# Loading K and V of two heads with one transfer in a decode attention kernel

## The chip, the cores and the metric

The kernel runs on one core of a Trainium2 chip; the chip's other cores are not used by it. The metric is device time in microseconds (us) of one execution. Three runs of the kernel before took 389.30, 389.39 and 389.51 us, median 389.39. A profile is one further execution, recorded by the hardware; its times are counted from its first instruction.

Engines are named as in the profile: PE does matrix products (PEld loads its stationary operand), DVE works on vectors, ACT evaluates functions, POOL does general work, and SP does nothing here but ask for transfers, in one fixed order.

## The reference

Four sequences decode one token each. The layer is attention over a window of the cache and then a gated feed-forward, both with a residual and a normalization without weights:

```
B, D = 4, 576;  Hq, Hkv, Sk, Dh = 32, 16, 16384, 128;  W = 4096;  F = 4608
q = (layernorm(x) @ wq)                        # 32 heads of 128
k = k_cache[:, :, Sk - W:, :]                  # bfloat16, each head serves two q heads
p = softmax(q . k * Dh**-0.5)                  # over the 4096 positions
h = x + (p . v) @ wo
gate, up = layernorm(h) @ W_gate, layernorm(h) @ W_up
out = h + (gate * (gate > 0) * up) @ W_down
```

There are 4 x 16 = 64 heads of K and of V, each 4096 x 128 in bfloat16, 1 MB. They are 134.2 MB of the 159.6 MB that the kernel reads; the rest are the five weight matrices. In memory the window of one head is contiguous, and two neighbouring heads of a sequence begin 16384 x 128 x 2 bytes = 4 MiB apart.

## The kernel before

The program for each engine is written out by hand. A small recorder (`Sched`, L48) notes which instruction signals what, and puts a semaphore wait in front of an instruction for each thing that it depends on. All transfers are asked for by SP in one list (`transfers`, L179, walked by `prog_sync`, L242): an entry first waits until the consumer of what its slot held before is done, and whatever stands behind it in the list waits with it.

The list is: wq in five pieces (L205 to L208); then for m from 0 to 68 K of head m (if there is one) and V of head m - 5 (`VLEAD`, L209 to L213); then wo in four pieces (L216), gate and up (L221, L226) and down (L234). K has a ring of six slots and V one of ten, each of 9216 bytes per partition, in one buffer, `pool` (L120). A slot of K comes free when the head has been transposed, one of V when its PV product is done. One K or V transfer is 1024 KB: partition p takes positions 32p to 32p + 31 of the head, a run of 8192 bytes (L195 to L203). wo comes with two runs of 4608 bytes per partition, gate and up with one run of 9216.

One head goes through these steps:

- **K transpose** (`tr`, L376, the instruction at L382): DVE transposes the 32 x 32 blocks of the head, seen as float32 pairs, from the slot into one of three buffers `kT` (`NKT`). It waits for the data and for the scores of three heads earlier.
- **Scores** (`qk`, L497): eight matmuls of 512 columns add up in two PSUM banks. Four heads form a batch n (`NB`): the stationary operand `qz` of a head is zero but for the columns of its own two q heads, so that the four heads of a batch accumulate into the same two banks on different rows. There are two such pairs of banks, `sc[0]` and `sc[1]` (L167), used in turn: batch n waits for the exponentials of batch n - 2.
- **Maximum and bias** (`rmax` L384, `fbias` L391): DVE takes the maximum of 1024 columns, masks it (`pmax`), POOL combines the partitions (L268), and DVE forms `t` and the `bias`, one number per row.
- **Exponentials** (L314): ACT, two of 512 columns each, with their sums.
- **P transpose** (`trp`, L397): DVE, and two small operations for the row sums; then ACT copies the result to `prob` as bfloat16 (L321).
- **PV** (`pv`, L514): eight matmuls of 512 columns per head, `PVLAG` = 6 heads behind the scores. After four heads ACT copies the result (`cpy`, L297), and `ext` (L526) picks out what belongs to each head.

The order on PE is: scores of head i, then (at a batch's start `ext` of the batch before) PV of head i - 6. The order on DVE around a batch is: K transpose of the batch's last head, maximum and `pmax`; K transpose of the next head, `t` and `bias`; K transpose of the head after, P transpose and row sums. So DVE does one K transpose while POOL works and another while ACT works.

The recorder issues all matmuls from one line, so that nearly all of PE's rows show L469; scores write `sc`, PV and `ext` write `pb`.

After the last batch come the normalized output (`norm`, L406), its product with wo, the second normalization, gate, up and down, all with the weights as the moving or stationary operand in `pool`; the transfers of down wait for the end of the product with wo, since they overwrite its slots.

Of the kernel before, what the change touches and what calls it, by code (L numbers as in the profile page):

```python
# [19 lines left out]
T = WIN // 128  # L20
# [3 lines left out]
NPAIR = B * KVH  # L24
NB = 4
NBATCH = NPAIR // NB
# [3 lines left out]
SLOT = 4608  # L30
NKS = 6
NVS = 10
NSLOT = NKS + NVS
# [3 lines left out]
PVLAG = 6  # L37
# [63 lines left out]
def bass_sequential_preLN__sliding_block_cached__glu_gated_reglu__decode_kernel(  # L101
# [12 lines left out]
    with ExitStack() as es:  # L114
# [4 lines left out]

        pool = sb("pool", [128, NSLOT, SLOT], BF16)  # L120
        kT = sb("kT", [128, NKT, WIN // 2], FP32)
# [20 lines left out]
        mask = sb("mask", [128, 4, 2 * NB], FP32)  # L142
        selT = sb("selT", [128, 4, 2 * NB], FP32)
        rmx = sb("rmx", [128, 2], FP32)
        pmax = sb("pmax", [128, 2, 2 * NB], FP32)
        bcm = sb("bcm", [128, 2, 2 * NB], FP32)
        t8 = sb("t8", [128, 2 * NB], FP32)
        bias = sb("bias", [128, 2], FP32)
        rs2 = sb("rs2", [128, 2, 2], FP32)
# [3 lines left out]
        prob = sb("prob", [128, 3, NB, T, 2], BF16)  # L153
# [13 lines left out]
        sc = [es.enter_context(nc.psum_tensor(f"sc{i}", [128, 1024], FP32)) for i in range(2)]  # L167
        pb = [sc[0][:, 0:512], sc[0][:, 512:1024], sc[1][:, 0:512], sc[1][:, 512:1024]]
# [8 lines left out]
        rings = {"K": [list(range(NKS)), 0], "V": [list(range(NKS, NSLOT)), 0]}  # L177
        slot_user = {}
        transfers = []  # L179
        slot_of = {}  # L180

        def add(name, ring, consumer, make, fixed=None):
            if ring is not None:
                slots, i = rings[ring]
                s = slots[i % len(slots)]
                rings[ring][1] += 1
                free = slot_user.get(s)
                slot_user[s] = consumer
                key = f"slot{s}"
            else:  # L190
                s, free, key = fixed, None, "fix_" + str(name).replace("'", "").replace("(", "").replace(")", "").replace(", ", "_")
            slot_of[name] = s
            transfers.append((name, key, free, lambda e, s=s: make(e, s)))

        def kv(cache, i):  # L195
            b, kvh = divmod(i, KVH)
            return cache[b, kvh, SK - WIN:SK, :].rearrange("(p t) d -> p (t d)", p=128)

        def add_K(i):
            add(("K", i), "K", ("TR", i), lambda e, s: e.dma_start(out=pool[:, s, 0:WIN], in_=kv(A_k_cache, i)))  # L200

        def add_V(i):
            add(("V", i), "V", ("PV", i), lambda e, s: e.dma_start(out=pool[:, s, 0:WIN], in_=kv(A_v_cache, i)))  # L203

        for c in range(4):  # L205
            add(("wq", c), "V", "QMM", lambda e, s, c=c: e.dma_start(out=pool[:, s, 0:H * DH], in_=A_wq[c * 128:(c + 1) * 128, :]))
        add(("wq", 4), "V", "QMM", lambda e, s: e.dma_start(out=pool[:, s, 0:H * DH // 2],
                                                            in_=A_wq[512:576, :].rearrange("r (u n) -> (r u) n", u=2)))  # L208
        for m in range(NPAIR + VLEAD):  # L209
            if m < NPAIR:  # L210
                add_K(m)
            if m >= VLEAD:
                add_V(m - VLEAD)  # L213
        for g in range(NWO):
            add(("wo", g), "K", "ATTN",
                lambda e, s, g=g: e.dma_start(out=pool[:, s, :].rearrange("p (q x) -> p q x", q=2),  # L216
                                              in_=A_wo[g * 1024:(g + 1) * 1024, :].rearrange("(q p e) n -> p q (e n)", q=2, e=4)))
        for c in range(4):
            for kind, W in (("wg", B_W_gate), ("wu", B_W_up)):
                add((kind, c), "V", None,  # L220
                    lambda e, s, c=c, W=W: e.dma_start(out=pool[:, s, 0:F], in_=W[c * 128:(c + 1) * 128, :]))  # L221

        s4 = rings["V"][0][rings["V"][1] % NVS]
        for u, (kind, W) in enumerate((("wg", B_W_gate), ("wu", B_W_up))):
            transfers.append(((kind, 4), f"gu4_{u}", slot_user[s4],
                              lambda e, u=u, W=W: e.dma_start(out=pool[:, s4, u * HALF:(u + 1) * HALF],  # L226
                                                              in_=W[512:576, :].rearrange("r (u n) -> (r u) n", u=2))))
        wd_sb = pool[:, 0:NKS, :].rearrange("p s x -> p (s x)")[:, 0:FC * D].rearrange("p (g x) -> p g x", g=NG)
        WD = [(0, GD * JJ), (GD * JJ, 2 * GD * JJ)] + [(g * JJ, (g + 1) * JJ) for g in range(2 * GD, NG - 1)] + [(FC - JJ, FC - 1), (FC - 1, FC)]
        for k, (f0, f1) in enumerate(WD):  # L230
            g0, j0 = divmod(f0, JJ)
            g1, nj = (f1 // JJ, JJ) if f1 - f0 >= JJ else (g0 + 1, f1 - f0)
            transfers.append((("wd", k), f"wd{k}", "ATTN",
                              lambda e, g0=g0, g1=g1, j0=j0, nj=nj: e.dma_start(  # L234
                                  out=wd_sb[:, g0:g1, j0 * D:(j0 + nj) * D],
                                  in_=B_W_down[g0 * 128 * JJ:g1 * 128 * JJ, :].rearrange("(g p j) n -> p g (j n)", p=128, j=JJ)[:, :, j0 * D:(j0 + nj) * D])))
# [5 lines left out]
        def prog_sync(S):  # L242
            for name, key, free, make in transfers:
                S.dma("sync", make, key, deps=[free], name=land(name))
# [27 lines left out]
        def prog_act(S):  # L272
# [12 lines left out]
            def qzero(n):  # L285
                b, q = divmod(n, 4)
                for g in range(4):
                    deps = []
                    if g == 0:
                        deps = ["D_QR", "QZ0"] if n < 2 else [("QK", NB * (n - 2) + NB - 1)]  # L290
                    src = bass.AP(tensor=qrep, offset=32 * g * 4 * H * B + 8 * q * B + b, ap=[[4 * H * B, 32], [2 * B, NB], [H * B, 4], [B, 2]])
                    dst = bass.AP(tensor=qz, offset=32 * g * 2 * NB * 512 + (n % 2) * NB * 512 + 32 * g,
                                  ap=[[2 * NB * 512, 32], [512 + 2, NB], [128, 4], [1, 2]])
# [11 lines left out]
            for n in range(NBATCH):  # L305
                for half in range(2):
                    deps = []
                    if half == 0:
                        deps = [("BIAS", n)]
                        if n >= 1:  # L310
                            deps.append(("TRP", n - 1))
                        if n >= 2:
                            deps.append(("RSUM", n - 2))
                    S.op(a, lambda e, n=n, half=half: e.activation(  # L314
                        out=P[:, half * 512:(half + 1) * 512], in_=sc[n % 2][:, half * 512:(half + 1) * 512], func=ACT.Exp,
                        scale=SCALE, bias=bias[:, n % 2:n % 2 + 1], accum_out=rs2[:, n % 2, half:half + 1]),
                        deps=deps, name=("EXP", n) if half else None, signal=half == 1)
                deps = [("TRP", n)]
                if n >= 3:
                    deps.append(("PV", NB * (n - 3) + NB - 1))  # L320
                S.op(a, lambda e, n=n: e.copy(out=prob[:, n % 3, :, :, :],  # L321
                                              in_=probT[:, :, 0:2 * NB].rearrange("p t (r h) -> p r t h", h=2)), deps=deps, name=("CMP", n))
# [13 lines left out]
        def prog_dve(S):  # L336
# [17 lines left out]
            for x in range(2):  # L354
                S.op(v, lambda e, x=x: e.memset(pb[PVB + x], 0.0), name=f"PVZ{x}")  # L355
            S.op(v, lambda e: e.tensor_reduce(out=mask[:, 0, :], in_=ident_b[:, :].rearrange("p (r u) -> p u r", u=2 * NB), axis=AX.X, op=ALU.add),
                 name="M0")
            S.op(v, lambda e: e.tensor_reduce(out=mask[:, 3, :], in_=bass.AP(tensor=ident_b, offset=0, ap=[[128, 128], [1, 2 * NB], [32, 4]]),
                                              axis=AX.X, op=ALU.add), name="M3")
# [3 lines left out]
                 name="M2")  # L363
            S.op(v, lambda e: e.reciprocal(out=st1[:, 5:6], in_=st1[:, 4:5]), deps=["A_STD"], name="D5")
# [11 lines left out]
            def tr(i):  # L376
                deps = [land(("K", i))]
                if i >= NKT:
                    deps.append(("QK", i - NKT))
                src = pool[:, slot_of[("K", i)], 0:WIN].bitcast(FP32).rearrange("p (t c k) -> p c t k", c=2, k=32)  # L380
# [3 lines left out]
            def rmax(n):  # L384
                S.op(v, lambda e: e.tensor_reduce(out=rmx[:, n % 2:n % 2 + 1], in_=sc[n % 2][:, :], axis=AX.X, op=ALU.max),  # L385
                     deps=[("QK", NB * n + NB - 1)], name=("RMAX", n))
                S.op(v, lambda e: e.tensor_scalar(out=pmax[:, n % 2, :], in0=mask[:, 1, :], scalar1=rmx[:, n % 2:n % 2 + 1], scalar2=None,  # L387
                                                  op0=ALU.min),
                     deps=[("RMAX", n), "M2"] + ([("PAR", n - 2)] if n >= 2 else []), name=("EMAX", n))

            def fbias(n):  # L391
                S.op(v, lambda e: e.scalar_tensor_tensor(out=t8[:, :], in0=bcm[:, n % 2, :], scalar=-SCALE, in1=mask[:, 2, :],  # L392
                                                         op0=ALU.mult, op1=ALU.max), deps=[("PAR", n)], name=("T8", n))
                S.op(v, lambda e: e.tensor_reduce(out=bias[:, n % 2:n % 2 + 1], in_=t8[:, :], axis=AX.X, op=ALU.min),  # L394
                     deps=[("T8", n)] + ([("EXP", n - 2)] if n >= 2 else []), name=("BIAS", n))

            def trp(n):  # L397
                S.op(v, lambda e: e.transpose(out=probT[:, :, :].rearrange("p t j -> p (t j)"), in_=P[:, :]),  # L398
                     deps=[("EXP", n)] + ([("CMP", n - 1)] if n >= 1 else []), name=("TRP", n))
                b, q = divmod(n, 4)  # L400
# [241 lines left out]
```

## Time and profile before

| | us |
|---|---|
| median of three runs | 389.39 |
| the profiled execution, its own time | 389.34 |
| its span, first to last instruction | 387.56 |
| PE busy | 301.1 (78%) |
| DVE busy | 204.6 (53%) |
| ACT busy | 60.1 (16%) |
| POOL busy | 10.7 (3%) |
| first scores begin | 27.48 |
| last K transpose begins | 320.34 |
| maximum of the last batch begins | 324.73 |
| last instruction group on PE (down) ends | 385.3 |

The times are of different things: the execution's own time is what is compared between kernels, the span is what the trace covers. In the trace, the views used are the page's 40 slices of the span (busy tenths of each engine, the granted PE clock, the DMA engines' share and the GB/s that they moved), the same by stretches of time, groups of instructions with their mean duration and what ended the idle time before them, the instructions in order of time, and the chain of waits, which is followed back from the last instruction to whatever released it. A transfer's time from its request to its landing (26.1 us for K and 26.9 us for V in the median) includes the queue in front of it.

### The profile page before, as it was taken

Reading aid. Unit: us, or ns where it says so; the run is one execution under the profiler, and the core shown is the slowest. Engines: PE = TensorE matmul, PEld = TensorE weight load, DVE = VectorE, ACT = ScalarE, POOL = GpSimd, SP = SyncE. Lnnn points to the kernel's source line nnn. Section 1 sums busy time; section 2 is a strip of 40 time slices with the busy share of each in tenths; the row PEclk is TensorE's granted clock in tenths of the full one; section 3 lists DMA queues with packets and bytes.
Section 4 is the critical chain, followed back from the end, with each engine's and each line's share of the span. In section 5 each row is a group of like instructions: output and inputs, shape, how many; then the busy total and the mean of one; then the engine's idle time right before and its main releaser. Section 6 shows DMA issues by size and latency. Waiting matters only on the chain.

```text
span 387.6 us, 4471 instructions
## 1 busy us (share of the span) xinstructions
PE 301.1 (78%) x1906; PEld 131.3 (34%) x1906; DVE 204.6 (53%) x228; ACT 60.1 (16%) x173; POOL 10.7 (3%) x28
## 2 busy tenths in 40 slices
PE   0078779797979797979787878796879798774477
PEld 0053224242424242324232323242323233364344
DVE  0265967658483856574748575656566665011000
ACT  4020212111111111111111111111111111200000
POOL 3000000000000000000000000000000000000000
PEclk9999699999989998989999999899989989875559
DMA  8999999999999999999999999999999999999995
GB/s 322 419 419 423 423 421 418 420 423 420 423 419 420 424 421 422 420 420 421 421 424 421 418 424 421 424 417 421 421 421 422 423 421 419 414 418 421 418 412 203
DMA packets 23524, 159.88 MB, mean 413 GB/s; under 512 B 2505, under 2 KB 2641, under 8 KB 5585
## 3 DMA queue, kind: packets, MB, share of 16 engines
q1 hardware_dynamic: 23496, 159.59, 99.3%
q8 instruction: 15, 0.25, 0.3%
q14 instruction: 5, 0.03, 0.0%
q10 hardware_dynamic: 8, 0.00, 0.0%
HBM read 159.58 MB, written 0.00 MB: 412 GB/s over the span
## 4 chain that ended last, share of the span: by engine, by line
DMA 55%; PE 26%; DVE 12%; issue 4%; SPq 1%; ACT 0%; POOL 0%; POOLq 0%
DMA pool<-in_A_k_cache_dram 42%; PE sc L469 15%; PE pb L469 11%; DVE kT L382 8%; DMA pool<-in_B_W_down_dram 7%; DMA pool<-in_A_wo_dram 6%; DVE rmx L385 2%; SPq L216 1%; DVE pmax L387 0%; DVE pb L355 0%; ACT qz L294 0%; ACT xn_bf L281 0%; DVE sel L346 0%; PE pb L476 0%; DVE qrep L416 0%
## 5 line engine op out<-in xcount | busy, mean ns | idle before, releaser
L382 DVE STREAM_TRANSPOSE kT<-pool 128x2048 f32<-128x2048 f32 x64 | 147.2, 2305 | 59.5 <-DMA pool<-in_A_k_cache_dram 59.3
L469 PE MATMUL sc<-kT,qz 128*128 128x512 bf16 x512 | 137.8, 416 | 44.3 <-DVE t L392 33.0
L469 PE MATMUL pb<-pool,prob 128*8 128x512 bf16 x512 | 120.2, 393 | 0.0
L469 PEld LDWEIGHTS sc<-kT,qz 128*128 128x128 bf16 x512 | 47.0, 101 | 130.6 <-DVE t L392 40.5
L469 PEld LDWEIGHTS pb<-pool,prob 128*8 128x8 bf16 x512 | 38.9, 88 | 73.7 <-issue 28.2
L314 ACT ACTIVATE P<-sc,bias 128x512 f32<-128x512 f32 x32 | 21.7, 683 | 160.6 <-DVE bias L394 160.6
L385 DVE TENSOR_REDUCE rmx<-sc 128x1 f32<-128x1024 f32 x16 | 19.6, 1225 | 47.0 <-PE sc L469 47.0
L398 DVE STREAM_TRANSPOSE probT<-P 128x1024 f32<-128x1024 f32 x16 | 19.3, 1205 | 1.5 <-ACT P L314 1.5
L469 PEld LDWEIGHTS pb<-selT,cp 128*128 128x128 f32 x128 | 16.6, 191 | 6.6 <-ACT cp L301 4.2
L469 PE MATMUL pb<-selT,cp 128*128 128x8 f32 x128 | 15.4, 247 | 3.2 <-ACT cp L301 3.2
L301 ACT COPY cp<-pb 128x512 f32<-128x512 f32 x16 | 9.4, 586 | 53.5 <-PE pb L469 53.5
L469 PE MATMUL pb<-hnT,pool 128*128 128x4 bf16 x288 | 8.8, 167 | 9.8 <-DMA pool<-in_B_W_up_dram 5.2
L476 PE MATMUL pb<-ident_b,xn_bf 4*128 4x4 bf16 (+1 forms) x5 | 0.4, 175 | 19.6 <-ACT xn_bf L281 19.6
L294 ACT COPY qz<-qrep 32x32 bf16<-32x32 bf16 x64 | 13.9, 217 | 7.6 <-DVE qrep L416 7.0
L268 POOL PARTITION_ALL_REDUCE bcm<-pmax x16 | 5.9, 368 | 304.4 <-DVE pmax L387 304.4
L321 ACT CAST prob<-probT 128x256 bf16<-128x256 f32 x16 | 6.6, 414 | 44.6 <-DVE rs L401 44.6
L469 PEld LDWEIGHTS pb<-hnT,pool 128*128 128x128 bf16 x288 | 8.2, 104 | 10.3 <-DMA pool<-in_B_W_up_dram 5.4
L460 DVE TENSOR_TENSOR hhT<-pb,gate_sb 128x144 bf16<-128x144 f32 x1 | 0.3, 308 | 20.9 <-ACT gate_sb L330 20.9
L469 PE MATMUL pb<-pool,hhT 128*4 128x288 bf16 x72 | 10.0, 306 | 0.4 <-DMA pool<-in_B_W_down_dram 0.4
L469 PEld LDWEIGHTS pb<-pool,hhT 128*4 128x4 bf16 x72 | 6.3, 90 | 4.1 <-DMA pool<-in_B_W_down_dram 0.9
L469 PE MATMUL sc<-oX,pool 128*128 128x4 bf16 (+1 forms) x160 | 5.7, 170 | 1.6 <-DMA pool<-in_A_wo_dram 1.1
L476 PEld LDWEIGHTS pb<-ident_b,xn_bf 4*128 4x128 bf16 (+1 forms) x5 | 0.3, 107 | 19.6 <-ACT xn_bf L281 19.6
(93 smaller groups left out, 71.7 us busy)
## 6 DMA issues: line engine op xcount, KB each, us to landing
pool<-in_A_k_cache_dram SPq DMA_DIRECT2D x64, 1024.0 KB, 26.1
pool<-in_A_v_cache_dram SPq DMA_DIRECT2D x64, 1024.0 KB, 26.9
pool<-in_A_wo_dram SPq DMA_DIRECT2D x4, 1152.0 KB, 27.0
pool<-in_B_W_gate_dram SPq DMA_DIRECT2D x4, 1152.0 KB, 25.7
pool<-in_B_W_up_dram SPq DMA_DIRECT2D x4, 1152.0 KB, 24.4
pool<-in_A_wq_dram SPq DMA_DIRECT2D x4, 1024.0 KB, 7.9
pool<-in_B_W_down_dram SPq DMA_DIRECT2D x2, 1296.0 KB, 27.3
pool<-in_B_W_down_dram SPq DMA_DIRECT2D x5, 432.0 KB, 14.7
```

Source lines behind the costliest of these rows:

```text
L216: lambda e, s, g=g: e.dma_start(out=pool[:, s, :].rearrange("p (q x) -> p q x", q=2), in_=A_wo[g * 1024:(g + 1) * 1024, :].rearrange("(q p ...
L268: S.op(g, lambda e, n=n: e.partition_all_reduce(bcm[:, n % 2, :], pmax[:, n % 2, :], 128, bass_isa.ReduceOp.max), deps=deps, name=("PAR", n))
L294: S.op(a, lambda e, src=src, dst=dst: e.copy(out=dst, in_=src), deps=deps, name=("QZ", n) if g == 3 else None, signal=g == 3)
L301: S.op(a, lambda e: e.copy(out=cp[:, n % 2, :], in_=pb[PVB + n % 2]), deps=deps, name=("CP", n))
L314: S.op(a, lambda e, n=n, half=half: e.activation(out=P[:, half * 512:(half + 1) * 512], in_=sc[n % 2][:, half * 512:(half + 1) * 512], fun ...
L321: S.op(a, lambda e, n=n: e.copy(out=prob[:, n % 3, :, :, :], in_=probT[:, :, 0:2 * NB].rearrange("p t (r h) -> p r t h", h=2)), deps=deps, ...
L382: S.op(v, lambda e: e.transpose(out=dst, in_=src), deps=deps, name=("TR", i))
L385: S.op(v, lambda e: e.tensor_reduce(out=rmx[:, n % 2:n % 2 + 1], in_=sc[n % 2][:, :], axis=AX.X, op=ALU.max), deps=[("QK", NB * n + NB - 1 ...
L398: S.op(v, lambda e: e.transpose(out=probT[:, :, :].rearrange("p t j -> p (t j)"), in_=P[:, :]), deps=[("EXP", n)] + ([("CMP", n - 1)] if n ...
L460: S.op(v, lambda e: e.tensor_tensor(out=hhT[:, :, :], in0=pb[GUB][:, FC * B:2 * FC * B].rearrange("p (f b) -> p f b", b=B), in1=gate_sb[:, ...
L469: S.op(t, lambda e: e.matmul(o, lhsT=l, rhs=r, start=start, stop=stop, skip_group_check=skip), deps=deps, name=name, signal=name is not None)
L476: S.op(t, lambda e, c=c, w=w, src=src, base=base: e.transpose(out=tpv[0:w, base + c * 4:base + (c + 1) * 4], in_=src[0:B, c * 128:c * 128 ...
```

## The change

K and V of two neighbouring heads ("duo") come with one transfer of 2048 KB. Head s of the duo goes to the partitions 2p + s: a partition takes 64 positions of one head instead of 32, a run of 16384 bytes. `pool` holds four slots for K and four for V, each of 16384 bytes per partition; the list on SP now alternates K of duo m and V of duo m - 5. The K slot of a duo comes free with its second transpose. wo, gate, up and down lie where the slots were, at places of their own, and wait for every consumer of what they cover.

A duo is transposed in two halves by the same instruction as before (`tr(2d)`, `tr(2d + 1)`: positions, not heads). Since the partitions alternate between the heads, so do the columns of the scores. Each half of the positions has two banks, and four duos (eight heads) form a batch, in all four banks of `sc`. There is one set of banks only: the scores of the next batch wait for the exponentials of this one (`("EXP", n - 1, th)`, by half). A row is valid in every second column; the exponentials are four per batch, each over the 512 columns of one parity within a half, with a bias per parity that makes the other head's columns zero. The maximum is taken per parity over 2 x 1024 columns, the P transpose is twice as long, and there are eight batches instead of sixteen. PV is sixteen matmuls per duo, five duos behind the scores (`PVLAG` = 5), and `prob` has two buffers instead of three.

On DVE the order around a batch changes: after the maximum of a batch the bias follows at once, ahead of the next K transpose, and the P transpose follows after one K transpose.

```diff
-T = WIN // 128
+T = WIN // 64
-NPAIR = B * KVH
+NDUO = B * KVH // 2
 NB = 4
-NBATCH = NPAIR // NB
+NBATCH = NDUO // NB
-SLOT = 4608
-NKS = 6
-NVS = 10
+DUO = 2 * WIN * DH // 128
+NKS = 4
+NVS = 4
-PVLAG = 6
+PVLAG = 5
...
-        sc = [es.enter_context(nc.psum_tensor(f"sc{i}", [128, 1024], FP32)) for i in range(2)]
+        sc = es.enter_context(nc.psum_tensor("sc", [128, 2048], FP32))
...
+        def duo(cache, d):
+            b, m = divmod(d, KVH // 2)
+            return cache[b, 2 * m:2 * m + 2, SK - WIN:SK, :].rearrange("s (p t) d -> p s (t d)", p=64)
+        def add_K(d):
+            s = d % NKS
+            add(("K", d), f"kslot{s}", s * DUO, DUO, ("TR", 2 * d + 1),
+                lambda e, o: e.dma_start(out=o, in_=duo(A_k_cache, d)))
...
+                for th in range(2):
+                    for u in range(2):
...
+                        S.op(a, lambda e, n=n, th=th, u=u: e.activation(
+                            out=P[:, th * 1024 + u:(th + 1) * 1024:2], in_=sc[:, th * 1024 + u:(th + 1) * 1024:2], func=ACT.Exp,
+                            scale=SCALE, bias=bias[:, n % 2, u:u + 1], accum_out=rs2[:, n % 2, 2 * th + u:2 * th + u + 1]),
...
+                S.op(v, lambda e: e.tensor_reduce(out=rmx[:, n % 2, :], in_=sc[:, :].rearrange("p (x u) -> p u x", u=2), axis=AX.X, op=ALU.max),
+                     deps=[("QK", 2 * NB * (n + 1) - 1)], name=("RMAX", n))
...
+                S.op(v, lambda e: e.tensor_reduce(out=bmin[:, n % 2:n % 2 + 1], in_=t8[:, :], axis=AX.X, op=ALU.min),
+                     deps=[("T8", n)], name=("BMIN", n))
+                S.op(v, lambda e: e.tensor_scalar(out=bias[:, n % 2, :], in0=rsel[:, :], scalar1=bmin[:, n % 2:n % 2 + 1], scalar2=None, op0=ALU.min),
...
-                if pos == NB - 1:
+                n, pos = divmod(i, 2 * NB)
+                if pos == 2 * NB - 1:
                     rmax(n)
+                    fbias(n)
                 if pos == 0 and n >= 1:
-                    fbias(n - 1)
-                if pos == 1 and n >= 1:
                     trp(n - 1)
...
+                if r == 0:
+                    if th == 0:
+                        deps.append(("QZ", n))
+                    if n >= 1:
+                        deps.append(("EXP", n - 1, th))
...
-            for i in range(NPAIR + PVLAG):
-                if i < NPAIR:
-                    qk(i)
+            for i in range(NDUO + PVLAG):
+                if i < NDUO:
+                    qk(2 * i)
+                    qk(2 * i + 1)
                 if i >= PVLAG:
                     if (i - PVLAG) % NB == 0 and i - PVLAG >= NB:
                         ext((i - PVLAG) // NB - 1)
                     pv(i - PVLAG)
```

RSEL, which the bias uses, is formed once at the start from the mask, in two small operations.

## The prediction

> **What bounds the kernel now.** I read the page's 40 slices first, because they tell whether anything pauses that everything needs.
>
> ```profile
> PEclk9999699999989998989999999899989989875559
> DMA  8999999999999999999999999999999999999995
> GB/s 322 419 419 423 423 421 418 420 423 420 423 419 420 424 421 422 420 420 421 421 424 421 418 424 421 424 417 421 421 421 422 423 421 419 414 418 421 418 412 203
> ```
>
> The reader is to see that the DMA engines are at nine tenths from the second slice to the last but one, and that the rate hardly moves whatever the engines do. TensorE is busy 78% of the span, VectorE 53%. So the end is set by 159.6 MB at some 420 GB/s, and compute matters only if it lets the queue run dry, or if work is left after the last byte. The chain of waits agrees: 55% of it is DMA.
>
> Second, the rate by stage (start:end, width, busy time of PE, PEld, DVE, ACT, POOL, clock, DMA share, GB/s):
>
> ```profile
> 200.00:210.00 10.00, 7.40 (x34) 2.65 (x33) 6.70 (x9) 1.40 (x4) 0.36 (x1) 1.00 1.01 422
> 336.00:338.00 2.00, 1.94 (x12) 0.63 (x8) 0.00 (x0) 0.02 (x1) 0.00 (x0) 0.88 1.02 412
> 338.00:340.00 2.00, 1.30 (x10) 1.19 (x10) 0.05 (x1) 1.85 (x2) 0.00 (x0) 1.00 1.02 412
> ```
>
> At 200 us K and V move: 1024 KB transfers, one run of 8192 bytes per partition (L200, L203). At 336 us wo moves: 1152 KB, two runs of 4608 bytes per partition (L216). The DMA is full in both, yet shorter runs go slower. It isn't transfer size: wo's transfers are larger.
>
> Third, one period of four heads in the chain in order of time (start, us, what), at full clock:
>
> ```profile
> 88.55 1.24 DVE rmx L385
> 89.81 0.23 DVE pmax L387
> 90.05 2.21 DVE kT L382
> 92.32 1.98 PE sc L469 x8
> 94.30 1.82 PE pb L469 x8
> ...
> 101.76 2.61 PE pb L469 x16
> ...
> 106.33 1.24 DVE rmx L385
> ```
>
> From maximum to maximum it is 17.78 us, while the DMA needs 8.39 MB / 422 = 19.88 us for those four heads. Compute has 11% to spare, with scores double-buffered.
>
> **The gain: longer runs.** After the change a partition takes 16384 bytes in one run. One of 16 engines moves 422/16 = 26.375 bytes per ns, so 8192 bytes take 310.6 ns; at 412 (25.75) 4608 bytes take 179.0 ns. The difference, 131.6 ns for 3584 bytes, is 36.7 ns per 1000 bytes (36.72), which leaves 9.8 ns per run that bytes don't explain. A run of 16384 bytes is then estimated at 601.6 + 9.8 = 611.4 ns against 621.2 for two: 1.57% less. K and V are 134.2 MB, 318.0 us at 422: **5.0 us saved**. Bounds: nothing (the rate may have stopped rising at 8 KB: gate and up, with 9216-byte runs, land 1152 KB per 2.79 us at 355 to 369 us, which is 422.5) and 7.4 us (doubling the run gains the 2.4% again that 4608 to 8192 gained: 432 GB/s). I take 5.0, from the two stages where the DMA alone sets the pace.
>
> The Trainium skill, "DMA: Bandwidth & Descriptors", section Bandwidth, gives about 2 us fixed per DMA plus the bytes at 436 GB/s. If that summed, 64 fewer transfers would save 128 us. The timeline shows K transposes waiting for data every 4.97 us for one K and one V, 422 GB/s, so the fixed part is already overlapped here and I take none of it.
>
> The same page, section "Latency and other measured facts", speaks against the change: copies with a row pitch of 4 MiB ran at 103 GB/s. The two heads of one transfer lie 16384 x 128 x 2 bytes = 4 MiB apart. By that figure K and V alone would take 1303 us. No row of this trace has such a step; within a head the rows follow each other at 16 KB.
>
> **Small changes off the path.** Matmuls stay 512 + 512 of 512 columns, K transposes 64, elements of maximum, exponential and P transpose the same in half as many, twice as long groups. RSEL (two operations) and one more operation per bias (some 0.2 us) are added on DVE, busy 53%. The prob copy has four times the elements in half as many copies: 414 ns becomes about 1.05 us by 0.83 ns per element, on ACT, busy 16%. Start and tail: wq is still first; the first scores wait for qz at 27.48, long after K0 has landed.
>
> **The cost: one score buffer instead of two.** The next batch's scores now wait for this batch's exponentials, and on DVE the bias comes before the next K transpose. Its parts, from the last batch, where nothing stood between:
>
> ```profile
> 325.99 0.23 DVE L387 TENSOR_SCALAR pmax<-mask,rmx 128x8 f32<-128x8 f32 x1
> 326.32 0.36 POOL L268 PARTITION_ALL_REDUCE bcm<-pmax  x1 [19.52 <-DVE pmax L387]
> 326.71 0.17 DVE L392 SCALAR_TENSOR_TENSOR t<-bcm,mask 128x8 f32<-128x8 f32 x1 [0.49 <-POOL bcm L268]
> 326.92 0.16 DVE L394 TENSOR_REDUCE bias<-t 128x1 f32<-128x8 f32 x1
> 327.11 0.69 ACT L314 ACTIVATE P<-sc,bias 128x512 f32<-128x512 f32 x1 [8.77 <-DVE bias L394]
> 327.79 0.68 ACT L314 ACTIVATE P<-sc,bias 128x512 f32<-128x512 f32 x1
> 328.59 1.25 DVE L398 STREAM_TRANSPOSE probT<-P 128x1024 f32<-128x1024 f32 x1 [1.52 <-ACT P L314]
> ```
>
> Count from the end of a batch's last scores. DVE: maximum of 2048 elements 0.1 to 2.43 (1.23 for 1024, 1.04 ns each); pmax to the next step 0.72, as above: 3.15; two small steps of 0.21: 3.57; K transpose 3.75 to 6.06. PE meanwhile has one PV group of 16 matmuls (2 x 1.82 = 3.64), then idles until 6.1: **2.46 us**. Scores end at 8.0. ACT: four exponentials at 0.68 from 3.8, done at 6.65; P's transpose to 9.0, two row-sum steps to 9.3, and only then the next K transpose, to 11.6, for which PE idles from 8.0: **3.65 us**. Behind that transpose on DVE stand all later K transposes, and SP's next K requests wait for them; behind the waiting scores on PE stand the next PV and ext, and SP's V requests, in one order with the K's, wait for PV.
>
> PE's work for eight heads: 8 x 1.91 + 8 x 1.82 + 0.79 for ext (2.61 - 1.82) + 0.12 = 30.8; with both pauses **36.9 us**. Clock: after a pause of 1.98 us the chain at 110 us shows scores and PV at 2.63 + 2.77 instead of 1.91 + 1.82: 1.67 us more. I charge that once per period: **38.5**. The DMA's new period is 39.76 x 0.9843 = 39.1. So compute stays under it, by 0.6 us instead of 4.2.
>
> Does it let the queue run dry? First scores at 27.48; the transposes follow at 2.3, so the first eight heads are scored at about 44.5, the next eight 38.5 later less one PV group and ext (4.4), at 78.6, the last at 78.6 + 6 x 38.5 = 309.6. PV of duo 26 of 0 to 31 then frees the slot of V30, 3.6 later, at 313.2. Before, the last K landed at 320.3 and five V followed at 2.49: 332.8; after, 5.0 earlier, 327.8, so the DMA comes to V30 9.8 before that: 318. Spare: 4.8 us. At the start, K4 is asked for after the second transpose, at about 29, when 13.1 MB are queued from 2 to 33. The tail (wo, gate, up, 36 us of DMA) hides the last PVs.
>
> **Sum.** The profiled execution took 389.34 us (span 387.56, 1.78 around it), the median of the runs is 389.39: the same. 389.34 - 5.0 = **384.3 us**.
>
> **Rivals.**
> 1. *Compute becomes the bound* (slower). Place: scores waiting for the exponentials and for the K transpose behind P's. It decides from a period of (318 - 3.6 - 78.6)/6 = 39.3; above that each us costs 6. Exponentials and maximum now read every second PSUM element. For DVE the row `L442`, a strided read, speaks for full rate: 199 ns for 40 elements, where 1225 ns for 1024 imply 200. For ACT no row shows it. At half rate on ACT each exponential takes 0.43 more: period 40.2, second batch at 80.3, PV 26 at 325.1, 7.1 late: 391.4. With the maximum at half rate too, 2.3 more: period 42.5, second batch at 82.6, PV 26 at 341.2, 23.2 late: 407.5. I price it at 393.
> 2. *The run length brings nothing*: 389.3. For: gate and up at 422.5 with runs of 9216 bytes. Against: the fit gives only 423.5 for these, too little more to tell the two apart, and 4608 to 8192 did gain.
> 3. *Two heads per transfer are read worse than one.* No row; bounded by the slowest long-run stage, 412: 134.2 MB / 412 = 325.7, 7.7 more: 397. The good end is the forecast.
>
> **Numbers.** Forecast 0.64, rival 1 0.14, rival 2 0.12, rival 3 0.10. Faster by over 0.2% (about what a measurement of this kernel can tell from no change) 0.64, within 0.12, slower 0.24. Range: 381.5 (the upper bound 7.4, rounded out) to 391.5, which takes in rival 2 and rival 1 with slow ACT reads; left out are 397 and most of rival 1, under 0.2.
>
> **What would show it.** Right: GB/s of 427 to 430 in the K and V slices, every slice still full, PE idle in pairs of about 2.5 and 3.7 us per eight heads. The run-length step is wrong if the K and V slices still say 422; rival 3 if they say less with the DMA share full; rival 1 if the DMA share falls below 9 in the middle or near V30, with the maximum near 4.6 us or an exponential near 1.1 us. The clock charge is wrong if scores at half clock take more than one group per period.

## The result, and the profile after

The changed kernel took 385.02 us (median of 4 runs, 384.69 to 385.30) against 389.37 us for the kernel before (4 runs, 389.30 to 389.51): ratio 0.9888, 95% interval 0.9870 to 0.9905, so 4.35 us less, with an interval of 3.7 to 5.1 us. The profiled execution took 385.30 us, its span 383.5 us. The forecast was 384.3. Ratios here and below are formed without runs that lie over 1.5% above the fastest of their kernel, which leaves out three of the ten runs of slack2 and no others.

The page's slices of the changed kernel, in the lines that were read first for the kernel before:

```profile
PEclk9999958998999899989998999899989998955559
DMA  7999999999999999999999999999999999999994
GB/s 316 426 424 426 431 424 432 426 424 431 426 424 434 424 427 431 426 427 431 426 427 434 424 424 434 427 424 432 427 424 434 426 423 434 403 417 424 414 415 172
```

The DMA is as full as before from the second slice to the last but one, but the slices of K and V say 423 to 434 GB/s where they said 417 to 424. Slices 35 to 39, the weights, whose transfers were not changed, say 403 to 424 against 412 to 421. By stage (start:end, width, busy time of PE, PEld, DVE, ACT, POOL, clock, DMA share, GB/s):

```profile
200.00:240.00 40.00, 31.56 (x136) 12.74 (x138) 25.94 (x22) 6.39 (x15) 0.39 (x1) 0.96 1.01 428
...
326.00:330.00 4.00, 3.74 (x22) 1.38 (x19) 0.00 (x0) 0.00 (x0) 0.00 (x0) 1.00 0.95 392
330.00:334.00 4.00, 3.44 (x16) 1.36 (x16) 0.00 (x0) 0.00 (x0) 0.00 (x0) 1.00 1.02 412
```

K and V run at 428 GB/s (422 before), wo at 412 as before. After the start, only the stretch from 326 to 330, where the last V ends and wo begins, shows the DMA not quite full.

The chain of waits has changed its face: PE 41%, DMA 23%, issue 15%, DVE 14%, where DMA had 55%. Here is one period of eight heads in the chain, in order of time (start, us, what):

```profile
191.69 2.30 DVE rmx L397
...
195.39 2.86 ACT P L323 x8
...
198.27 2.31 DVE probT L413
...
200.89 2.23 DVE kT L394
...
203.16 3.57 PE sc L482 x8
206.73 3.55 PE pb L482 x16
210.28 3.73 PE sc L482 x16
...
226.48 34.38 DMA pool<-in_A_k_cache_dram
```

No transfer stands in this chain until 226: compute alone paces the heads from the first batch to there, because it starts behind. Yet the slices show a full DMA all the while: the requests run ahead by as much as the slots hold. A chain that says 41% PE over a DMA that is full is a lag being made up, not a bound. From 226 on the chain runs through the K transfers. (K transposes waited for data before that too, up to 5.28 us, but PE still had work then, so these waits are not in the chain.)

### The profile page after: what moved, and what is told of

Same layout as the page of the kernel before. It is cut to its first block, busy times and chain, and to the rows that moved or that the text cites. A ratio compares the mean times of both kernels' runs of the same rounds, so it can differ in the third digit from the quotient of the medians.

```text
span 383.5 us, 4157 instructions
## 1 busy us (share of the span) xinstructions
PE 288.7 (75%) x1827; PEld 130.2 (34%) x1842; DVE 198.8 (52%) x181; ACT 51.5 (13%) x125; POOL 7.9 (2%) x20
## 4 chain that ended last, share of the span: by engine, by line
PE 41%; DMA 23%; issue 15%; DVE 14%; ACT 5%; POOL 1%; SPq 0%; POOLq 0%
PE sc L482 23%; PE pb L482 18%; DMA pool<-in_A_k_cache_dram 9%; DMA pool<-in_B_W_down_dram 7%; DMA pool<-in_A_wo_dram 7%; ACT P L323 4%; DVE kT L394 4%; DVE probT L413 4%; DVE rmx L397 4%; POOL bcm L274 1%; DVE bias L409 0%; DVE rowsum L418 0%; DVE t L405 0%; DVE pmax L400 0%; DVE bmin L407 0%
## 5 line engine op out<-in xcount | busy, mean ns | idle before, releaser
L482 PE MATMUL sc<-kT,qz 128*128 128x512 bf16 x497 | 131.9, 418 | 51.2 <-DVE kT L394 47.6
L482 PE MATMUL pb<-pool,prob 128*16 128x512 bf16 x512 | 116.4, 386 | 0.8 <-DMA pool<-in_A_v_cache_dram 0.8
L482 PEld LDWEIGHTS pb<-pool,prob 128*16 128x16 bf16 x512 | 43.5, 91 | 71.0 <-issue 15.3
L397 DVE TENSOR_REDUCE rmx<-sc 128x2 f32<-128x2048 f32 x8 | 18.3, 2292 | 34.0 <-PE sc L482 34.0
L413 DVE STREAM_TRANSPOSE probT<-P 128x2048 f32<-128x2048 f32 x8 | 18.5, 2311 | 7.8 <-ACT P L323 7.8
L308 ACT COPY cp<-pb 128x512 f32<-128x512 f32 x8 | 4.7, 584 | 67.5 <-PE pb L482 67.5
L482 PE MATMUL pb<-selT,cp 128*128 128x16 f32 x64 | 7.9, 255 | 4.3 <-ACT cp L308 4.3
L330 ACT CAST prob<-probT 128x1024 bf16<-128x1024 f32 x8 | 8.4, 1044 | 19.0 <-DVE rs L416 19.0
L482 PEld LDWEIGHTS pb<-selT,cp 128*128 128x128 f32 x64 | 8.2, 191 | 6.3 <-ACT cp L308 5.3
L301 ACT COPY qz<-qrep 32x64 bf16<-32x64 bf16 x32 | 7.8, 245 | 7.3 <-DVE qrep L431 7.0
## 6 DMA issues: line engine op xcount, KB each, us to landing
pool<-in_B_W_down_dram SPq DMA_DIRECT2D x5, 432.0 KB, 14.5
```

Of the source, the lines that this page charges most:

```text
L301: S.op(a, lambda e, src=src, dst=dst: e.copy(out=dst, in_=src), deps=deps, name=("QZ", n) if g == 3 else None, signal=g == 3)
L308: S.op(a, lambda e: e.copy(out=cp[:, n % 2, :], in_=pb[PVB + n % 2]), deps=deps, name=("CP", n))
L330: S.op(a, lambda e, n=n: e.copy(out=prob[:, n % 2, :, :, :], in_=probT[:, :, 0:NHB].rearrange("p t (r x) -> p r t x", x=4)), deps=deps, na ...
L397: S.op(v, lambda e: e.tensor_reduce(out=rmx[:, n % 2, :], in_=sc[:, :].rearrange("p (x u) -> p u x", u=2), axis=AX.X, op=ALU.max), deps=[( ...
L482: S.op(t, lambda e: e.matmul(o, lhsT=l, rhs=r, start=start, stop=stop, skip_group_check=skip), deps=deps, name=name, signal=name is not None)
```

## The experiments

The theory: a run of 16384 bytes per partition costs less DMA time than two of 8192, the DMA sets the end, and the slower compute of one score buffer stays hidden. The rivals: the gain is that of larger or fewer transfers; the step of 4 MiB between the two heads costs something that the gain outweighs; compute is already the bound, so that any more of it is paid in full. Kernels that were timed in one execution only are marked so. The kernel before took 389.23 to 389.59 us (medians) when timed beside them.

### Loads alone

Six kernels keep nothing but the transfers of K and V, through a ring of slots as large as the kernels', each slot waiting for its own last landing; all computing and all weights are left out, and the output is a copy of x. They differ in how one transfer is laid out; the core of each:

```python
# d8:     1 MB of one head, one run of 8192 bytes per partition
cache[b, h, SK - WIN:SK, :].rearrange("(p t) d -> p (t d)", p=128)
# d8x2:   2 MB of two heads, two runs of 8192
cache[b, 2 * m:2 * m + 2, SK - WIN:SK, :].rearrange("s (p t) d -> p s (t d)", p=128)
# d16:    2 MB of two heads, one run of 16384 (the change)
cache[b, 2 * m:2 * m + 2, SK - WIN:SK, :].rearrange("s (p t) d -> p s (t d)", p=64)
# d16one: 2 MB of one head, one run of 16384, no step of 4 MiB
cache[b, 2 * m, SK - 2 * WIN:SK, :].rearrange("(p t) d -> p (t d)", p=128)
# d4:     1 MB of one head, two runs of 4096
cache[b, h, SK - WIN:SK, :].rearrange("(s p t) d -> p s (t d)", s=2, p=128)
# d32:    4 MB of four heads, one run of 32768, four slots
cache[b, 4 * m:4 * m + 4, SK - WIN:SK, :].rearrange("s (p t) d -> p s (t d)", p=32)
```

d16one reads 2 MB that are not the window's in part, but as many bytes in all.

> Loads only: K and V of all heads with 128 transfers of 1 MB, one run of 8192 bytes per partition, 16 slots; no attention, no feed-forward is computed, and the output is x. Both theories expect the rate of the kernel before: 134.2 MB at 422 GB/s = 318 us, and some 5 us around it, about 323 us.

> Loads only, nothing is computed: 64 transfers of 2 MB, two runs of 8192 bytes per partition. Theory run length (each run costs 9.8 ns beside 36.7 ns per 1000 bytes): the same 422 GB/s as with 1 MB transfers, within 0.5 us of them. Rival transfer size (fewer and larger requests are what helps): the 428 GB/s of the changed kernel, some 5 us less than with 1 MB transfers.

> Loads only, nothing is computed: the transfers of the changed kernel, 2 MB of two heads, one run of 16384 bytes per partition. Theory run length: 428.6 GB/s, 4.9 us less than with runs of 8192 bytes, whatever their transfers' size. Rival transfer size: the same as two runs of 8192 bytes in 2 MB.

> Loads only, nothing is computed: 2 MB per transfer, one run of 16384 bytes per partition, but all of one head (8192 positions in a row), so that no step of 4 MiB is in it; the data are other ones of the caches. If the step of 4 MiB between the two heads costs something, this is faster than the two-head transfers; theory run length expects the same time within 0.5 us.

> Loads only, nothing is computed: 1 MB transfers with two runs of 4096 bytes per partition. Theory run length: 4096 bytes take 150.4 + 9.8 ns on each of 16 engines, 409 GB/s, 10 us more than with runs of 8192. Rival transfer size: as with one run of 8192 in 1 MB.

> Loads only, nothing is computed: 4 MB transfers of four heads, one run of 32768 bytes per partition, four slots. Theory run length: 32768 bytes take 1203.3 + 9.8 ns, 432 GB/s, 2.5 us less than with runs of 16384. Rival: no more gain once a run has 16384 bytes.

| one execution each | run, bytes | transfer | us | GB/s from 100 to 200 us |
|---|---|---|---|---|
| d4 | 4096 | 1 MB | 333.99 | 410 |
| d8 | 8192 | 1 MB | 324.49 | 422 |
| d8x2 | 8192 | 2 MB | 324.58 | 422 |
| d16 | 16384 | 2 MB | 320.04 | 429 |
| d16one | 16384 | 2 MB, one head | 319.86 | 428 |
| d32 | 32768 | 4 MB | 317.16 | 433 |

The rate in the middle of the run, d8 first and d16 second (start:end, width, POOL, clock, DMA share, GB/s):

```profile
100.00:200.00 100.00, 0.00 (x0) 1.00 1.01 422
```

```profile
100.00:200.00 100.00, 0.00 (x0) 1.00 1.01 429
```

With nothing else on the core the rates are those of the full kernels' K and V slices, 422 and 428. At equal runs, doubling the transfer changes 0.09 us (d8, d8x2); at equal transfers, doubling the run takes 4.54 us off (d8x2, d16); without the step between two heads it is 0.18 us less (d16one). So the run's length is what counts. The profile's packet counts go with it: d8 has 18449 packets, 2064 of them under 8 KB, and d16 has 9232, 1040 of them under 8 KB, which leaves one packet per run in both. Halving the number of runs saves 9.5 us from d4 to d8 and 4.45 from d8 to d16. 134.2 MB are 16384 runs of 8192 bytes, 1024 per DMA engine; half of these fewer is 512, and 4.45 / 512 = 8.7 ns per run. From d4 to d8 it is 9.5 / 1024 = 9.3 ns, from d16 to d32 2.88 / 256 = 11.2. Single executions do not settle whether these differ.

### The whole kernel with short runs in the same large transfers

runs8 is the changed kernel, its slots, requests, order and engines' work untouched, but a partition takes two runs of 8192 bytes from two heads instead of one of 16384. The positions then lie elsewhere than the computation takes them to be: the instructions are the same, the output isn't the reference's.

```diff
-            ... .rearrange("s (p t) d -> p s (t d)", p=64)
+            ... .rearrange("s (p t) d -> p s (t d)", p=128)
...
-                lambda e, o: e.dma_start(out=o, in_=duo(A_k_cache, d)))
+                lambda e, o: e.dma_start(out=o.rearrange("p (s x) -> p s x", s=2), in_=duo(A_k_cache, d)))
```

> The changed kernel with one thing undone: its 2 MB transfers bring each partition two runs of 8192 bytes (one of each head) instead of one of 16384. The data lie in other places than the scores assume, so the output is not the reference's; every instruction and wait is the same. Theory run length: the K and V rate falls back to 422 GB/s and the time to 385.0 + 4.9 = 389.9 us, level with the kernel before. Rival transfer size or buffering: 385 us, as the changed kernel.

It took 389.81 us (10 runs, 389.27 to 390.11), ratio to the kernel before 1.0004 [0.9994, 1.0013]: the whole gain is gone. Its slices:

```profile
DMA  7999999999999999999999999999999999999995
GB/s 313 416 420 422 422 419 423 421 421 419 423 422 421 420 420 424 420 421 422 422 420 423 420 421 420 423 421 419 424 421 422 419 420 422 415 418 420 417 411 211
```

The DMA is as full as in the changed kernel and moves 419 to 424 GB/s, the kernel before's rate. All the rest of the change together (fewer requests, new order, one score buffer, half as many batches) is worth nothing, within 0.13%, in either direction.

### More compute per batch

Three kernels add work to DVE in the place that holds up the next batch: one more maximum over scores, unread, ahead of the real one. slack1 reads 1024 columns, slack2 2048, slack4 does that twice: 1.22, 2.29 and 4.57 us per batch by their rows.

```diff
+                for k in range(1):                      # slack4: range(2)
+                    S.op(v, lambda e, k=k: e.tensor_reduce(out=rscr[:, k, :],
+                             in_=sc[:, 0:1024].rearrange("p (x u) -> p u x", u=2),   # slack2, slack4: 0:2048
+                             axis=AX.X, op=ALU.max),
+                         deps=[("QK", 2 * NB * (n + 1) - 1)], name=("XMAX", n, k))
```

> The changed kernel with one more maximum over 1024 elements ahead of each batch's maximum, whose result nobody reads: 1.23 us more on the path from the last scores of a batch to the next. The trace of the changed kernel has a compute period of 37.8 us per eight heads. Theory (compute is hidden, and shows only when PV of duo 26 ends after the DMA asks for V30's slot, at about 319 us): period 39.0, PV 26 at 308.8 + 7 x 1.23 = 317, no change, 385.0. Rival (compute is already the bound): 8 x 1.23 = 9.8 us more, 395.

> The same with one more maximum over 2048 elements, 2.29 us per batch. Theory: period 40.1, PV 26 at 308.8 + 7 x 2.29 = 324.8, 6 us late, so about 391 us. Rival (compute is already the bound): 8 x 2.29 = 18 more, 403. If nothing changes, the point from which compute decides lies higher than I worked out.

> The same with two more maxima over 2048 elements, 4.58 us per batch. Theory: PV 26 at 308.8 + 7 x 4.58 = 340.9, 22 us late, so about 407 us. Rival (compute is already the bound): 8 x 4.58 = 37 more, 422.

| | added per batch | median us (runs) | ratio to before | period | last scores end | V30's slot free against 318 |
|---|---|---|---|---|---|---|
| changed kernel | 0 | 385.02 (4) | 0.9888 | 38.23 | 307.6 | 6.8 early |
| slack1 | 1.22 | 385.86 (4) | 0.9903 [0.9882, 0.9924] | 38.94 | 314.2 | 0.2 early |
| slack2 | 2.29 | 390.0 (10) | 0.9969 [0.9934, 1.0004] | 39.84 | 319.2 | 4.8 late |
| slack4 | 4.57 | 406.46 (4) | 1.0447 [1.0405, 1.0489] | 42.0 | 333.5 | 19.1 late |

The period is from the maximum of the second batch to that of the last, over six; the last column adds 3.6 us for one PV to the end of the last scores and takes off the 318 at which the prediction had the DMA come to V30. slack2's ten runs spread from 385.54 to 395.76; by its ratio it takes 388.3 us beside 389.46, and its profiled execution, from which its period and slices come, took 391.48.

The slices of slack2, then of slack4:

```profile
DMA  8999999999999999999999999999999888999995
GB/s 318 422 429 429 431 427 425 426 427 425 426 431 429 427 431 429 425 427 424 431 425 427 429 429 429 431 431 427 425 429 424 342 333 306 414 417 422 417 411 200
```

```profile
DMA  8999999999999999999999999989994578999994
GB/s 320 428 423 430 431 425 433 422 435 420 432 425 431 423 430 426 428 425 431 430 426 426 375 423 435 425 328 399 426 438 179 209 282 316 421 416 422 418 411 196
```

In slack2 the DMA moves 424 to 431 from the third slice to the 31st and falls to 306 to 342 in slices 32 to 34, 302 to 331 us: the requests for the last V's are waiting for slots, the place that the prediction's first rival named. In slack4 it falls to 179. PE's timeline of slack2 shows what they wait for (start, us, what, count):

```profile
315.47 3.80 PE L486 MATMUL sc<-kT,qz 128*128 128x512 bf16 x16
319.19 6.22 PE L486 MATMUL pb<-pool,prob 128*16 128x512 bf16 x32
```

The PV of duo 26, behind the last scores, begins at 319.2; V30 needs its slot. The rival "already bound" fell: 1.22 us more per batch, eight times, cost 0.8 us, not 10. From slack2 on each us is paid six to eight times: 2.28 us more per batch cost 14.5 us between the two profiled executions, 406.46 - 390.0 = 16.5 by the medians and 18.6 by the ratios. The hidden reserve is real and small: slack1, with a period of 38.9, is at its edge (one slice, the 34th, falls to 353 GB/s), and at 39.8 it is spent.

### The last microsecond: a cold PE at the end?

In the changed kernel the down product, PE's last work, took half a microsecond longer than before (10.55 against 10.05), and the granted clock was 0.50 to 0.53 for the first 3 us of it; in the kernel before it began at 0.50 as well, but had 0.64 in the next 2 us (376 to 378). Two kernels try to keep the clock up with unread matmuls of 512 columns into a bank (of PSUM) that nothing reads: warm has five behind each of the eight large gate and up pieces, warm2 also seven just ahead of the down product.

```diff
+                    for _ in range(5):
+                        mm(pb[3], ident_b[:, :], pool[:, s:s + 512], True, True, skip=True)
...
+            for _ in range(7):                          # warm2 only
+                mm(pb[3], ident_b[:, :], pool[:, at[("wu", 3)]:at[("wu", 3)] + 512], True, True, skip=True)
```

> The changed kernel with five more matmuls of 512 columns after each of the eight large pieces of gate and up, whose result nobody reads, so that PE is not idle between the pieces. Theory: the down product runs 10.5 us because the granted clock is at half in its first 2.2 us (8.6 us at full clock by 72 x 120 ns) and ends 2.4 us after the last byte; with PE kept busy it ends about 1 us earlier, 384 us. Rival: the last landing sets the end, and the time stays at 385.0, or rises if the added matmuls hold up gate and up.

> The kernel with five unread matmuls behind each of the eight large gate and up pieces, and seven more unread ones just ahead of the down product, where PE stood idle 1.33 us and the down product then began at a granted clock of 0.56. Theory A (the last microsecond that the change did not bring is a down product that starts at half clock): 18 matmuls per 2 us at full clock are 0.111 us each, 72 take 8.0 us instead of 10.55; from 370.5 that is before the last byte (378.8), so the landing sets the end, some 0.5 us after it; 1.5 us less than the 385.0 of the kernel without the seven: 383.5. Theory B (the down product is paced by its weights' landing): its duration stays 10 us or more at a full clock, and the time stays at 385.0.

warm took 385.02 us (4 runs, 384.35 to 385.22; ratio 0.9879 [0.9864, 0.9894]), warm2 385.29 (6 runs, 384.47 to 387.02; ratio 0.9904 [0.9882, 0.9926]). Neither is a gain. PE's end in the changed kernel, in warm and in warm2 (start, us, what, count, idle time before and its releaser):

```profile
368.10 2.17 PE L482 MATMUL pb<-ident_f,R_sb 128*4 128x128 f32 x12
...
370.69 10.54 PE L482 MATMUL pb<-pool,hhT 128*4 128x288 bf16 x72 [0.42 <-DMA pool<-in_B_W_down_dram]
```

```profile
367.82 1.24 PE L482 MATMUL pb<-ident_f,R_sb 128*4 128x128 f32 x12
370.40 10.55 PE L482 MATMUL pb<-pool,hhT 128*4 128x288 bf16 x72 [1.33 <-DMA pool<-in_B_W_down_dram]
```

```profile
369.12 1.69 PE L482 MATMUL sc<-pool,ident_b 128*128 128x512 bf16 x7
370.74 2.37 PE L482 MATMUL pb<-pool,hhT 128*4 128x288 bf16 x18
373.71 6.89 PE L482 MATMUL pb<-pool,hhT 128*4 128x288 bf16 x54 [0.60 <-DMA pool<-in_B_W_down_dram]
```

warm missed its own aim: the clock was 1.00 from 360 to 370, but PE then finished early, stood idle 1.33 us, and the down product ran at 0.56 to 0.59 for 4 us again. warm2 has the clock at 1.00 to the end, and shows what stands behind: PE now waits 0.60 us for the second piece of down (373.71), and the 54 matmuls behind it take 6.89 us, 128 ns each. The 111 ns of theory A came from counting matmuls in windows of 2 us, where those on the border count twice. From 370.74 the whole product took 9.86 us, near the 10 of theory B. The end came at 380.60 against 381.24 in the profiles, 0.6 us earlier, and the six runs, half of them above 385.8, show nothing of it. So the cold clock at the end is worth 0.6 us at most, and that the missing part of the gain went there is not shown.

## Why the prediction was right, point by point

**The bound.** DMA throughout, before and after; the loads alone show 422 and 429 GB/s without any compute.

**The gain, 5.0 us.** Right in cause, 0.6 us too large. The rate came out as worked out: 611.4 ns per run is 16384 x 16 / 611.4 = 428.8 GB/s, the trace has 428. At 422 and 428.5 the 134.2 MB differ by 4.8 us, and the loads alone save 4.45. In the profiled executions of the two kernels the last V lands 4.7 us earlier (330.5 against 335.3), the down product begins 4.55 us earlier, and the execution ends 4.04 us earlier, the down product being 0.5 us longer. In the loads alone the start looks slower: from 2 to 4 us d8 moves at 270 GB/s and d16 at 180, 90 x 2 / 429 = 0.4 us, while SP takes about 0.6 us for each of its first requests instead of 0.4. But d8x2 starts like d16 (188) and still ends 0.09 us from d8, so the start is not shown to be what is missing. The kernel's own 4.35 agrees with 4.45; with an interval of 3.7 to 5.1 us, which takes in the 5.0, nothing that is left needs a cause. Of the bounds, "nothing" fell with runs8 and d8x2 against d16; 7.4, a rate of 432, is what d32 has with runs of 32768.

**A fixed cost per transfer.** d8 and d8x2, 128 transfers and 64 for the same bytes, differ by 0.09 us: queued back to back, none of a fixed cost showed, as the prediction chose. The Trainium skill, "DMA: Bandwidth & Descriptors", has about 2 us per DMA, in its section "Anatomy of one DMA — SWDGE (gpsimd) path" (the prediction names the section Bandwidth) and for transfers that GpSimd asks for, where SP asks here; summed, it would be an estimated 128 us.

**The step of 4 MiB.** d16 and d16one, with and without the step of 4 MiB, differ by 0.18 us, and both run at 428 to 429 GB/s. The same page's 103 GB/s at a pitch of 4 MiB (section "Latency and other measured facts") was given for copies between tensors in HBM, in which every partition lies one pitch from the next; here two heads lie 4 MiB apart, each read in runs of 16384 bytes, and nothing slows. Rival 3 fell, and rival 2 with runs8.

**Small changes off the path.** As costed: the prob copy takes 1044 ns (1.05 predicted), and the strided reads of PSUM, for which the kernel before had no row of ACT, go at nearly full rate. The groups of the changed kernel (form, count, busy us, mean ns, idle before):

```profile
L323 ACT ACTIVATE P<-sc,bias 128x512 f32<-128x512 f32 x32 | 22.2, 714 | 176.5 <-DVE bias L409 176.5
L413 DVE STREAM_TRANSPOSE probT<-P 128x2048 f32<-128x2048 f32 x8 | 18.5, 2311 | 7.8 <-ACT P L323 7.8
L397 DVE TENSOR_REDUCE rmx<-sc 128x2 f32<-128x2048 f32 x8 | 18.3, 2292 | 34.0 <-PE sc L482 34.0
```

The exponential takes 714 ns against 683, the maximum of 2048 elements 2.29 us against 2 x 1.225. Both ways in which rival 1 could have come true by half rate fell.

**One score buffer.** The two pauses of PE per eight heads were worked out as 2.46 and 3.65 us. PE's timeline of the changed kernel:

```profile
197.86 1.75 PE L482 MATMUL sc<-kT,qz 128*128 128x512 bf16 x7 [2.65 <-DVE kT L394]
203.16 3.57 PE L482 MATMUL sc<-kT,qz 128*128 128x512 bf16 x8 [3.56 <-DVE kT L394]
```

They are 2.65 and 3.56, both ended by the K transposes that the steps named, and the clock charge is there once per period: eight matmuls in 3.57 us at half clock instead of 1.91, 1.66 against 1.67. In the three periods before, the slow stretch runs on into the PV group behind it (2.95 + 4.17, 3.10 + 4.02 and 3.44 + 3.66 us in the chain), but scores and PV together take 7.10 to 7.12 us each time, as here. The period where compute paces is 37.8 us (maxima at 78.36, 116.08, 154.01, 191.69, 229.64), 0.7 under the 38.5: sixteen matmuls in a row take 3.73 and 3.55 in the chain, not twice the 1.91 and 1.82 of rows of eight. So the second batch's maximum came at 78.36 (78.6 predicted) and the last's at 307.74 (309.6).

**The queue not running dry.** Right in its outcome: V30's slot came free 6.8 us ahead of 318 instead of 4.8, and a period of 39.3 lies between slack1, which pays next to nothing, and slack2, which pays. But that 318 fits is partly luck. The sum has five V's behind the last K, where the list has six (V58 to V63), each 2.49 us. The last V of the kernel before was asked for at 308.53 and landed 26.7 us later, at 335.3, where the sum had 332.8 (start, us, what; then KB, us to landing):

```profile
308.53 2.13 SPq L203 DMA_DIRECT2D pool<-in_A_v_cache_dram  x1
pool<-in_A_v_cache_dram SPq DMA_DIRECT2D x1, 1024.0 KB, 26.7
```

So the DMA of the changed kernel comes to V30 only when V29 lands, at 320.7. On the other side, the sum let a slot be free at the moment at which the DMA comes to it, and the request has to be earlier. In slack2, V29 is asked for at 315.56, half a microsecond before V28 lands (316.1):

```profile
315.56 0.54 SPq L211 DMA_DIRECT2D pool<-in_A_v_cache_dram  x1
pool<-in_A_v_cache_dram SPq DMA_DIRECT2D x1, 2048.0 KB, 7.5
```

It takes 7.5 us to land, where the V's of the changed kernel land 4.9 us after each other. In slack1, V30 is asked for at 317.8, 2.9 us before V29's landing at 320.7, and V31 lands at 330.5 as in the changed kernel. An estimate from these rows is that a request has to be some 7.5 - 4.9 = 2.6 us ahead, so that the slot must be free at about 318.1: the V too few and the lead left out, some 2.5 us each, cancel. In slack2's trace V31 lands at 336.1, 5.6 us later than in the changed kernel, and the execution is 6.2 us longer; in slack4's it lands at 349.9, 19.4 us later (19.1 by the sum), and the execution is 20.7 us longer. What was lost behind the last V, 0.6 to 1.3 us in the three slack traces, was not followed.

**The tail.** PE waited 0.82 us for V31 (until 330.56), and the DMA moved 392 GB/s at 326 to 330, which is some 0.3 us ((428 - 392) x 4 / 428). The sum had no term for it, nor for the start, where the first scores came at 28.67 instead of 27.48; that one stayed hidden, as the second batch was on time.

## What to carry to other kernels

Where a DMA queue stays full through the whole kernel, look at the length of the contiguous run per partition before the size of the transfer (1 MB and 2 MB made no difference here): every run cost some 9 to 11 ns per engine beside its bytes, so that doubling runs of 8 KB gave 1.4% of the time of K and V and doubling again 0.9%. Work out, before paying for longer runs with buffers, how much later compute may come: the slots hide a lag of a few us in total, after which each us per batch is paid once per batch. The chain of waits cannot tell these apart; the DMA share by slice can.

## What the runs showed of the hardware that was not expected

A low granted clock followed a pause of only 1.33 us: in warm the clock was 1.00 until 370, PE stood idle from about 369.1 to 370.4, and the next 4 us ran at 0.56 to 0.59; in warm2, with seven matmuls in that pause, the clock stayed at 1.00. On the other hand eight matmuls after a pause of 2.65 us, in the middle of the changed kernel, ran at full speed (7 in 1.75 us), and those after the next pause, 3.56 us, did not (8 in 3.57). The length of the last pause alone does not tell which it will be.

Transfers of 4 MB in four slots (d32) did not run evenly: slices of 449 and 416 GB/s take turns, and still the time is the shortest of all, 317.16 us.

slack2, whose reserve is just spent, spread over 10 us from run to run (385.54 to 395.76), while the changed kernel stays within 0.6 and slack4 within 3.7. What differed between its runs was not found.

A transfer that is asked for when the queue has just run empty shows a delay that the full queue hides: 7.5 us for 2 MB in slack2 (7.6 to 7.9 for V27 to V30 in slack4), where 2 MB take 4.9 us in a full queue.
